# Recurrence outputs formed transposed, two heads at a time in the two halves of the array, with the chunk decay sent through DRAM

## The chip, the cores and the metric

The kernel runs on one core of one Trainium2 chip. The metric is the device time of one execution in microseconds (us). Before the change the median of 3 runs is 918.32 us (907.49 to 930.42).

## The reference, cut to what matters

Two parts follow each other. A gated linear recurrence runs over 4 sequences of 768 steps with 8 heads of 48 elements; its output, 3072 tokens of 384 elements, goes through a two-level top-1 mixture of 16 experts.

```python
# gated recurrence, per batch and head; a = a_re + i a_im, made at most 0.999 long
for t in range(S):
    S = a[t] * S + outer(k[t], v[t])        # S: 48 x 48, complex
    y[t] = q[t] @ real(S)
# mixture of experts over x = y by token, [3072, 384]
g = argmax(x @ w_group);  e = argmax(x @ w_expert[g])       # 4 groups of 4 experts
out = p_g * p_e * (relu(x @ w1[g, e]) @ w2[g, e])           # p: the softmax weights of the choice
```

All arrays are 32-bit floats; an expert's `w1` is 384 x 1024 and its `w2` 1024 x 384.

## The kernel before, in words

**Tiling.** The recurrence is worked off in 24 chunks of 128 steps, two chunks to a group, so 12 groups, three to a sequence. Within a chunk the decay and the turn of every step are running sums over the chunk (a product with a triangular matrix on TensorE); q and k are scaled and turned by them, and what is left are matrix products. A 96 x 384 state (`G`: cos and sin parts by 8 heads of 48) carries from chunk to chunk. The running sum of the log decay is measured from the middle of the chunk, so the state is multiplied by a half chunk's decay when it enters (`enter`, L405) and by the other half when it leaves (`leave`, L435).

**Steps of a group.** `gate_steps` (L285) makes the log decay (`ta`), the scales `E` and `Ei` (L311 to L320) and the angle (`tb`). Its step `decays` (L323) spreads `ta` over the cos and sin copies on GpSimd (L328) and multiplies each of 2 x 8 blocks with a 128 x 2 matrix `halves` on TensorE (L331), which gives the half chunks' decays in partitions; VectorE keeps their greatest (L334) and ScalarE takes the exponential `M` (L336). `turn_steps` (L352) makes sines and cosines and the products `Q` and `K`.

**Steps of a chunk** (`chunk_steps`, L396): `scores` transposes four heads of Q and K (L419, copied by ScalarE at L423 and VectorE at L425), multiplies them into `at` (L428) and masks it into `am` on VectorE (L431). `leave` forms the new state (L440 to L448). `outputs` (L451) forms y as 128 tokens x 384: per head one matmul with the 128 x 128 `am` stationary and 48 columns of v moving (L456), and one with the 96 x 128 `QT` stationary and 48 columns of the entering state moving (L458). ScalarE copies y to `x` (L461) and at once sends it to `x_dram` (L463). `gating` transposes x in three blocks (L183 in `transposed`, called by `gate`), VectorE copies them to `xT` (L188), and three matmuls against `wg` give the logits (L191, L192). `route` (L204), a group later, chooses the experts and writes the table of tokens.

**Order of the work.** The five engines and the DMA queues each run their own instructions in order and wait on semaphores. A loop over groups calls `weave` (L18), which mixes the step lists of four groups by a fraction of the iteration; a scheduler of the framework then sets each engine's order. SyncE issues the loads of q, k, v, a_re, a_im, and of the first two experts' weights; ScalarE issues the writes of `x_dram`.

```python
for g in range(-1, NG):
    turn, product = turned(g + 1)
    main = [f for c in range(GC) for f in chunk_steps(g, c)] if g >= 0 else []
    weave((0.0, 1.0, main), (0.0, 0.6, gates(g + 2)), (0.1, 0.1, routed(g - 1)),
          (0.0, 0.5, turn), (0.61, 1.0, product))
```

So the scales and decays of a group are made two iterations before its chunks use them. After the last group a branch tests whether any half chunk decayed by more than `exp(-LIMIT)`; if so, a loop would step through the recurrence in time. It isn't entered with these inputs. Then come the experts, each with its first 256 tokens (L626 and L635), and a loop for tokens beyond.

Of the kernel before, what the change touches and what calls it, by code (L numbers as in the profile page):

```python
# [10 lines left out]
F32 = mybir.dt.float32  # L11
# [16 lines left out]
def tile_gateloop_moe(  # L28
# [43 lines left out]
    NP = H // 2                 # head pairs  # L72
# [3 lines left out]
    LIMIT = 27.0  # L76
# [22 lines left out]
    table = dp.tile([NE * N, 2], I32, name="table")  # L99

# [9 lines left out]
    halves = cp.tile([P, 2], F32, name="halves")  # L110
    nc.vector.memset(halves, 0.0)
    nc.vector.memset(halves[0:64, 0:1], 1.0)
    nc.vector.memset(halves[64:128, 1:2], 1.0)
    lmat = cp.tile([P, P], F32, name="lmat")
    nc.vector.tensor_scalar(out=lmat, in0=ut, scalar1=-1.0, scalar2=halves[:, 0:1], op0=ALU.mult, op1=ALU.add)
# [12 lines left out]
    wg = cp.tile([P, KD, NW], F32, name="wg")  # L128
    nc.scalar.dma_start(out=wg[:, :, 0:G], in_=w_group.rearrange("(i p) g -> p i g", p=P))
    for g in range(G):  # L130
        nc.scalar.dma_start(out=wg[:, :, G + g * Eg:G + (g + 1) * Eg],
                            in_=w_expert[g].rearrange("(i p) e -> p i e", p=P))
# [12 lines left out]
    # counted[e] is how many tokens so far chose expert e; empty slots of the table name row N,  # L145
    # which is zero and has no row of the result.
# [11 lines left out]
    decay_max = cp.tile([P, GC * H * 2], F32, name="decay_max")  # L158
    nc.vector.memset(decay_max, 0.0)
# [19 lines left out]
    def transposed(x, evac):  # L179
        """[128 tokens, DM] -> [128 d, KD, 128 tokens]."""  # L180
# [5 lines left out]
    def gate(x, gl, c):  # L186
        xT = rp.tile([P, KD, P], F32, tag="xT", name="xT")
        transposed(x, lambda tp: nc.vector.tensor_copy(out=xT, in_=tp))  # L188
        lg = bank("sm", [P, NW])
        for i in range(KD):  # L190
            nc.tensor.matmul(out=lg, lhsT=xT[:, i, :], rhs=wg[:, i, :], start=(i == 0), stop=(i == KD - 1))  # L191
        nc.vector.tensor_copy(out=gl[:, c, :], in_=lg)  # L192

    def choose(logits, sh, oh):
        """oh: one-hot of the first greatest logit; sh: logits less the greatest."""
# [8 lines left out]
    def route(g, gl):  # L204
# [14 lines left out]
        # weight: 1 / (sum of the groups' exponentials) / (sum of the experts')  # L219
# [9 lines left out]
        # rank within the expert: earlier tokens of the chunk, earlier chunks, earlier groups  # L229
# [55 lines left out]
    def gate_steps(g):  # L285
        """Scales, decays and angles of a group."""
# [14 lines left out]
        def log_decay():  # L301
            # nl = ln(mag + 1e-6) - ln(mag) - min(ln(mag), ln(0.999)), the gate's -log magnitude
# [20 lines left out]
        def decays():  # L323
            # a half chunk's whole decay, by (cos and sin x d, head)
# [395 lines left out]
```

## Time and profile before

| | |
|---|---|
| median of 3 runs | 918.32 us (907.49, 918.32, 930.42) |
| the profiled execution: span from first to last instruction | 922.2 us (what lies around the span is not listed for it) |
| TensorE (PE) busy | 801.3 us, 87% of the span |
| its weight loads (PEld) busy | 649.3 us, 70% |
| VectorE (DVE) busy | 412.0 us, 45% |
| ScalarE (ACT), GpSimd (POOL) busy | 208.9 us and 208.1 us, 23% each |
| mean granted clock of TensorE | 0.811 of full speed |

The span has three stages: a start of about 52 us, the recurrence from there to 519.6 us, and the experts from about 553 us, with a passage of 33 us between. A matmul of 32-bit floats stands in the trace as two records (x384 at L456 are 192 matmuls), a transpose as one. Records of one stream overlap, so a record's duration is longer than its distance to the next; "busy" in the table by stretch is the time in which at least one of the rows asked for was running. PEclk is the granted clock as a share of 2.4 GHz: 0.5 is 1.2 GHz, 1.0 is 2.4 GHz, and what lies between is a mean over a stretch.

### The profile page before, as it was taken

Reading aid. Unit: us, or ns where it says so; the run is one execution under the profiler, and the core shown is the slowest. Engines: PE = TensorE matmul, PEld = TensorE weight load, DVE = VectorE, ACT = ScalarE, POOL = GpSimd, SP = SyncE. Lnnn points to the kernel's source line nnn. Section 1 sums busy time; section 2 is a strip of 40 time slices with the busy share of each in tenths; the row PEclk is TensorE's granted clock in tenths of the full one; section 3 lists DMA queues with packets and bytes.
Section 4 is the critical chain, followed back from the end, with each engine's and each line's share of the span. In section 5 each row is a group of like instructions: output and inputs, shape, how many; then the busy total and the mean of one; then the engine's idle time right before and its main releaser. Section 6 shows DMA issues by size and latency. Waiting matters only on the chain. (4 is left out here: it accounts for less than half of the span.)

```text
span 922.2 us, 10483 instructions
## 1 busy us (share of the span) xinstructions
PE 801.3 (87%) x3953; PEld 649.3 (70%) x3953; DVE 412.0 (45%) x1019; ACT 208.9 (23%) x356; POOL 208.1 (23%) x214
## 2 busy tenths in 40 slices
PE   1578989899899999999999609999999999999994
PEld 0467878688878778788888507767777777777762
DVE  5486787857757757657563311121111111111110
ACT  2454434334242433342321100000000000000000
POOL 4541314313131503123010021122221111111000
PEclk9977677866656667576665659999999999999997
DMA  8812202122120203000000013455555554544400
GB/s 275 306 61 77 77 28 78 55 74 66 38 75 29 78 26 103 10 27 9 9 10 11 17 26 113 167 169 170 182 183 184 182 182 169 170 167 158 151 13 15
DMA packets 54011, 90.89 MB, mean 99 GB/s; under 512 B 10156, under 2 KB 45016, under 8 KB 53954
## 3 DMA queue, kind: packets, MB, share of 16 engines
q1 hardware_dynamic: 43488, 73.96, 24.5%
q0 software_dynamic: 4864, 11.04, 3.4%
q10 hardware_dynamic: 5602, 5.15, 1.6%
q8 instruction: 33, 0.54, 0.3%
q14 instruction: 24, 0.20, 0.1%
HBM read 80.28 MB, written 11.43 MB: 99 GB/s over the span
## 5 line engine op out<-in xcount | busy, mean ns | idle before, releaser
L626 PE MATMUL cs<-xgT,w 128*128 128x256 f32 x768 | 171.2, 383 | 8.1 <-DVE xgT L621 8.1
L626 PEld LDWEIGHTS cs<-xgT,w 128*128 128x128 f32 x768 | 145.5, 191 | 31.1 <-DVE xgT L621 11.7
L631 ACT ACTIVATE hT<-cs 128x256 f32<-128x256 f32 x64 | 24.6, 384 | 344.8 <-PE cs L626 344.8
L456 PE MATMUL y<-v,am 128*128 128x48 f32 x384 | 89.9, 336 | 9.3 <-DVE am L431 9.2
L456 PEld LDWEIGHTS y<-v,am 128*128 128x128 f32 x384 | 78.4, 256 | 19.7 <-DVE am L431 13.6
L629 DVE TENSOR_SCALAR hT<-cs 128x256 f32<-128x256 f32 x64 | 27.2, 425 | 144.9 <-PE cs L626 141.9
L428 PE MATMUL at<-QT,KT 96*128 96x128 f32 x384 | 82.3, 380 | 7.5 <-DVE am L431 2.4
L639 POOL DMA_INDIRECT out_dram<-ot,ent x32 | 32.5, 1014 | 242.2 <-DVE ot L638 238.2
L635 PE MATMUL at<-w,hT 128*128 128x384 f32 x256 | 85.2, 486 | 0.0
L635 PE MATMUL y<-w,hT 128*128 128x384 f32 x256 | 85.2, 486 | 0.0
L428 PEld LDWEIGHTS at<-QT,KT 96*128 96x128 f32 x384 | 71.9, 278 | 15.2 <-DVE KT L425 7.0
L458 PE MATMUL y<-Gp,QT 96*128 96x48 f32 x320 | 77.8, 332 | 0.0
L635 PEld LDWEIGHTS y<-w,hT 128*128 128x128 f32 x256 | 48.6, 190 | 33.9
L635 PEld LDWEIGHTS at<-w,hT 128*128 128x128 f32 x256 | 48.6, 190 | 30.5
L328 POOL COPY both<-ta 128x768 f32<-128x768 f32 x24 | 24.3, 1037 | 200.0 <-DVE mx L201 116.7
L458 PEld LDWEIGHTS y<-Gp,QT 96*128 96x128 f32 x320 | 64.8, 251 | 0.0
L314 PE MATMUL cs<-ta,lmat 128*128 128x384 f32 x48 | 33.4, 849 | 25.1 <-DVE ta L308 24.8
L246 POOL DMA_INDIRECT table<-pay,slot_i x24 | 27.7, 1152 | 117.9 <-DVE slot_i L244 52.8
L419 PE MATMUL tp<-ident,K 128*96 128x128 f32 x192 | 42.5, 359 | 9.9 <-ACT QT L423 9.9
L610 POOL DMA_INDIRECT xg<-x_dram,ent x32 | 32.8, 1024 | 62.5 <-PE tp L183 49.4
L423 ACT COPY QT<-tp 96x512 f32<-96x512 f32 x48 | 27.9, 582 | 77.1 <-PE tp L419 72.3
L431 DVE TENSOR_TENSOR am<-at,mask 128x512 f32<-128x512 f32 x48 | 33.1, 689 | 26.9 <-PE at L428 26.2
(143 smaller groups left out, 1150.5 us busy)
## 6 DMA issues: line engine op xcount, KB each, us to landing
w<-in_w_dram SPq DMA_DIRECT2D x32, 1536.0 KB, 7.3
ar<-in_a_re_dram SPq DMA_DIRECT2D x12, 384.0 KB, 4.2
ai<-in_a_im_dram SPq DMA_DIRECT2D x12, 384.0 KB, 3.7
q<-in_q_dram SPq DMA_DIRECT2D x12, 384.0 KB, 3.9
k<-in_k_dram SPq DMA_DIRECT2D x12, 384.0 KB, 4.8
v<-in_v_dram SPq DMA_DIRECT2D x12, 384.0 KB, 3.2
x_dram<-x ACTq DMA_DIRECT2D x24, 192.0 KB, 2.4
xg<-x_dram,ent POOLq DMA_INDIRECT x32, 5.0
```

What stands on the lines that cost most here:

```text
L246: nc.gpsimd.indirect_dma_start(out=table, out_offset=bass.IndirectOffsetOnAxis(ap=slot_i[:, c:c + 1], axis=0), in_=pay[:, c, :], in_offset ...
L314: nc.tensor.matmul(out=cs, lhsT=lmat, rhs=t["a"][:, c], start=True, stop=True)
L419: nc.tensor.transpose(out=tp[:, j, :], in_=T[nm, g, c][:, hg * 4 + j].rearrange("p u d -> p (u d)"), identity=ident)
L423: nc.scalar.copy(out=tr[nm][0:DD], in_=tp)
L428: nc.tensor.matmul(out=at[:, j, :], lhsT=tr["K"][0:DD, j, :], rhs=tr["Q"][0:DD, j, :], start=True, stop=True)
L431: nc.vector.tensor_tensor(out=am, in0=at, in1=mask4, op=ALU.mult)
L456: nc.tensor.matmul(out=yh, lhsT=z["am", hg][:, j, :], rhs=V(h), start=True, stop=first)
L458: nc.tensor.matmul(out=yh, lhsT=z["QT", hg][0:DD, j, :], rhs=z["Gp"][0:DD, h, :], start=False, stop=True)
L610: nc.gpsimd.indirect_dma_start(out=xg, out_offset=None, in_=x_dram, in_offset=bass.IndirectOffsetOnAxis(ap=idx, axis=0), bounds_check=N, o ...
L626: nc.tensor.matmul(out=h, lhsT=wa[:, i, f * P:(f + 1) * P], rhs=xT[:, i, :], start=(i == 0), stop=(i == KD - 1))
L635: nc.tensor.matmul(out=y, lhsT=hT[:, f, i * P:(i + 1) * P], rhs=wb[:, f, :], start=(f == 0), stop=(f == KF - 1))
L639: nc.gpsimd.indirect_dma_start(out=out, out_offset=bass.IndirectOffsetOnAxis(ap=entries[i][:, 0:1], axis=0), in_=ot, in_offset=None, bound ...
```

## The change

- The log decay is summed from the chunk's start (`lmat` is the negated triangular matrix alone), ScalarE reads the sums from PSUM without the clamp on VectorE, and `LIMIT` doubles.
- The last row of `E`, the decay of a whole chunk, is written to `decay_dram` by SyncE, and read back two times per group into the 96 partitions of `decay`, 48 x 16 single elements each. The GpSimd copies, the L331 matmuls, the greatest on VectorE and the exponential `M` are gone.
- The state is multiplied once, when it leaves; `enter` is gone.
- `outputs` forms y transposed: v (or the state) is stationary, 64 or 48 columns of it, and `am` (or `QT`) moves with 128 columns. The even head of a pair goes to partitions 0 to 63, the odd one to 64 to 111, so each uses one half of the array's columns. Per chunk it is 16 matmuls as before (8 in a sequence's first chunk).
- ScalarE copies 112 x 512 instead of 128 x 384. The logits come from this transposed form directly, with four matmuls against a `wg` that is laid out by pairs of heads, with zeros between.
- For `x_dram`, four transposes turn the copy back; VectorE copies them to `x`, and ScalarE's DMA follows that copy.

```diff
-    lmat: tensor_scalar(in0=ut, scalar1=-1.0, scalar2=halves[:, 0:1], op0=ALU.mult, op1=ALU.add)
+    lmat: tensor_scalar(in0=ut, scalar1=-1.0, scalar2=None, op0=ALU.mult)
...
-    wg = cp.tile([P, KD, NW], F32, name="wg")
-    nc.scalar.dma_start(out=wg[:, :, 0:G], in_=w_group.rearrange("(i p) g -> p i g", p=P))
+    wg = cp.tile([P, NP, NW], F32, name="wg")
+    nc.vector.memset(wg, 0.0)
+    for u in range(2):
+        rows = slice(u * 64, u * 64 + D)
+        nc.scalar.dma_start(out=wg[rows, :, 0:G], in_=w_group.rearrange("(n u d) g -> u d n g", n=NP, u=2)[u])
...
         def scales(c):
...
-                cl = tp_.tile([P, DM], F32, tag="cl", name="cl")
-                nc.vector.tensor_scalar(out=cl, in0=cs, scalar1=LIMIT, scalar2=-LIMIT, op0=ALU.min, op1=ALU.max)
                 for nm, sg in (("E", 1.0), ("Ei", -1.0)):
                     e = tp_.tile([P, DM], F32, tag=f"{nm}{c}", name=f"{nm}{c}")
-                    act(out=e, in_=cl, func=AF.Exp, scale=sg)
+                    act(out=e, in_=cs, func=AF.Exp, scale=sg)
                     T[nm, g, c] = e
+                nc.sync.dma_start(out=decay_dram[g * GC + c:g * GC + c + 1, :], in_=T["E", g, c][P - 1:P, :])
             return f
 
         def decays():
-            ms = bank("sm", [DD, GC * H, 2])
-            for c in range(GC):
-                both = pp.tile([P, H, 2, D], F32, tag="both", name="both")
-                nc.gpsimd.tensor_copy(out=both, in_=t["a"][:, c].rearrange("p (h d) -> p h d", d=D).unsqueeze(2)
-                                      .to_broadcast([P, H, 2, D]))
-                for h in range(H):
-                    nc.tensor.matmul(out=ms[:, c * H + h, :], lhsT=both[:, h].rearrange("p u d -> p (u d)"),
-                                     rhs=halves, start=True, stop=True)
-            dm = decay_max[0:DD].rearrange("p (a b) -> p a b", b=2)
-            nc.vector.tensor_tensor(out=dm, in0=ms, in1=dm, op=ALU.max)
-            M = st.tile([P, GC * H, 2], F32, tag="M", name="M", bufs=4)
-            act(out=M[0:DD], in_=ms, func=AF.Exp, scale=-1.0)
+            rows = decay_dram[g * GC:(g + 1) * GC, :].rearrange("c (h d) -> d (c h)", d=D)
+            with nc.allow_non_contiguous_dma(reason="rows to partitions"):
+                for u in range(2):
+                    nc.sync.dma_start(out=decay[u * D:(u + 1) * D, g * GC:(g + 1) * GC, :]
+                                      .rearrange("d c h -> d (c h)"), in_=rows)
...
         def leave():
+            z["G"] = T["G"] if not first else None
...
-            M2 = T["M", g][0:DD, c * H:(c + 1) * H, 1:2].to_broadcast([DD, H, D])
+            M = decay[0:DD, g * GC + c, :].unsqueeze(2).to_broadcast([DD, H, D])
...
         def outputs():
-            y = bank("y", [P, DM])
-            for h in range(H):
-                hg, j = divmod(h, 4)
-                yh = y[:, h * D:(h + 1) * D]
-                nc.tensor.matmul(out=yh, lhsT=z["am", hg][:, j, :], rhs=V(h), start=True, stop=first)
-                if not first:
-                    nc.tensor.matmul(out=yh, lhsT=z["QT", hg][0:DD, j, :], rhs=z["Gp"][0:DD, h, :],
-                                     start=False, stop=True)
-            x = st.tile([P, DM], F32, tag="x", name="x")
-            nc.scalar.copy(out=x, in_=y)
-            r0 = g * TG + c * P
-            nc.scalar.dma_start(out=x_dram[r0:r0 + P, :], in_=x)
+            y = bank("y", [P, NP, P])
+            vs = T["v", g][:, c]
+            gs = None if first else z["G"][0:DD].rearrange("p h d -> p (h d)")
+            for n in range(NP):
+                both = [(h, slice(u * 64, u * 64 + w), slice(h * D, h * D + w))
+                        for u, (h, w) in enumerate(((2 * n, 64), (2 * n + 1, D)))]
+                for h, rows, cols in both:
+                    nc.tensor.matmul(out=y[rows, n], lhsT=vs[:, cols], rhs=z["am", h // 4][:, h % 4],
+                                     start=True, stop=first)
+                if not first:
+                    for h, rows, cols in both:
+                        nc.tensor.matmul(out=y[rows, n], lhsT=gs[:, cols], rhs=z["QT", h // 4][0:DD, h % 4],
+                                         start=False, stop=True)
+            xT = st.tile([P, NP, P], F32, tag="xT", name="xT")
+            nc.scalar.copy(out=xT[0:PR], in_=y[0:PR])
+            z["xT"] = xT
 
         def gating():
+            xT = z["xT"]
+            tp = bank("tp", [P, NP, P], 2)
+            for n in range(NP):
+                nc.tensor.transpose(out=tp[:, n, 0:PR], in_=xT[0:PR, n, :], identity=ident[0:PR, 0:PR])
+            x = st.tile([P, NP, 2, D], F32, tag="x", name="x")
+            nc.vector.tensor_copy(out=x, in_=tp.rearrange("p n (u r) -> p n u r", u=2)[:, :, :, 0:D])
+            r0 = g * TG + c * P
+            nc.scalar.dma_start(out=x_dram[r0:r0 + P, :], in_=x.rearrange("p n u d -> p (n u d)"))
...
-            gate(z["x"], T["gl", g], c)
+            lg = bank("sm", [P, NW])
+            for n in range(NP):
+                nc.tensor.matmul(out=lg, lhsT=xT[0:PR, n, :], rhs=wg[0:PR, n, :], start=(n == 0), stop=(n == NP - 1))
+            nc.vector.tensor_copy(out=T["gl", g][:, c, :], in_=lg)
```

The changed kernel's lines carry other numbers: L311 is the sum of the log decay, L316 the write to `decay_dram`, L323 the read into `decay`, L440 and L444 the output matmuls, L447 ScalarE's copy, L454 the transposes back, L456 VectorE's copy, L458 the DMA to `x_dram`, L463 the logits.

On TensorE, the outputs of a chunk begin behind the transposes of its second four heads (`tp<-ident,K`) and the scores (`at`). `y` is the output bank, `am` the masked scores, `QT` the transposed q, `Gp` or `G` the state. Before:

```order
L419 MATMUL tp<-ident,K_558 96x128 x4
L428 MATMUL at<-QT,KT 128x128 x4
L456 MATMUL y<-v,am 128x48
L458 MATMUL y<-Gp,QT 128x48
L456 MATMUL y<-v,am 128x48
```

Now, in the first chunk of a middle group (a row is the output's partitions x columns; 64 and 48 partitions are the two halves):

```order
L407 MATMUL at<-QT,KT 128x128 x4
L398 MATMUL tp<-ident,K_826 96x128 x4
L440 MATMUL y<-am,v 64x128
L440 MATMUL y<-am,v 48x128
L444 MATMUL y<-QT,G 64x128
L444 MATMUL y<-QT,G 48x128
```

The two kinds alternated per head; now each kind comes as a pair of halves, and the next pair of heads follows.

On TensorE, the end of a group's first chunk before, from its last outputs to the next chunk's scores (`sm<-halves,both` are the decays, `tp<-ident,x` and `sm<-wg,xT` the gating):

```order
L458 MATMUL y<-Gp,QT 128x48
L360 MATMUL cs<-tb,tmat 128x384
L362 MATMUL cs<-f_726,last 128x384
L183 MATMUL tp<-ident,x 128x128 x3
L419 MATMUL tp<-ident,Q_598 96x128 x4
L331 MATMUL sm<-halves,both 96x2 x16
L419 MATMUL tp<-ident,K_602 96x128 x4
L191 MATMUL sm<-wg,xT 128x20 x3
```

Now:

```order
L444 MATMUL y<-QT,G 48x128
L454 MATMUL tp<-ident,xT 128x112 x4
L398 MATMUL tp<-ident,Q_867 96x128 x4
L311 MATMUL cs<-ta,lmat 128x384 x2
L398 MATMUL tp<-ident,K_871 96x128 x4
L398 MATMUL tp<-ident,Q_867 96x128 x2
L347 MATMUL cs<-tb,tmat 128x384
```

The sixteen decay matmuls are gone, there is one transpose more, and the logits (`sm<-wg,xT`, x4) come some rows later.

On ScalarE, the copy of the outputs and the DMA to `x_dram` in a middle group before:

```order
L176 ACT_TABLE_LOAD
L461 COPY x<-y 128x384
L463 DMA x_dram<-x 128x384
L423 COPY QT<-tp 96x512
L173 ACTIVATE ta<-ta 128x768
L173 ACTIVATE tb<-ta 128x768
```

Now:

```order
L181 ACT_TABLE_LOAD
L447 COPY xT<-y 112x512
L402 COPY QT<-tp 96x512
L178 ACTIVATE ta<-ta 128x768
L458 DMA x_dram<-x 128x384
L178 ACTIVATE tb<-ta 128x768
```

The DMA stands two instructions later, behind a wait for VectorE's copy of `x`.

## Rows read from the trace of the kernel before

**Rows 1.** Busy time by stretch of the span: stretch, length, each engine's busy us
```profile
core 0: us, PE busy (x) PEld busy (x) DVE busy (x) ACT busy (x) POOL busy (x), PEclk, DMA share, GB/s
52.00:106.80 54.80, 50.41 (x324) 43.52 (x323) 40.05 (x93) 22.10 (x36) 14.12 (x13) 0.78 0.15 47
106.80:434.60 327.80, 301.67 (x1717) 261.60 (x1715) 230.43 (x576) 119.99 (x195) 93.11 (x89) 0.68 0.18 54
454.90:519.60 64.70, 60.86 (x346) 56.01 (x344) 30.11 (x104) 11.76 (x20) 4.54 (x6) 0.66 0.03 10
```

**Rows 2.** Waits in 106.8 to 434.6 us: engine line <- released by: us, times, longest
```profile
DVE xT L188 <- PE tp L183: 19.3, 8, 4.7
...
PEld tp L419 <- ACT QT L423: 13.2, 16, 1.1
...
PEld y L456 <- DVE am L431: 9.5, 11, 1.2
```

**Rows 3.** Busy time by stretch, instructions on tile y alone (PE, PEld, DVE, ACT)
```profile
106.80:434.60 327.80, 78.33 (x464) 77.15 (x464) 0.00 (x0) 7.67 (x16) 0.68 0.18 54
454.90:519.60 64.70, 22.46 (x128) 21.45 (x128) 0.00 (x0) 1.44 (x4) 0.66 0.03 10
```

**Rows 4.** The same, instructions of line 428 alone (PE, PEld)
```profile
106.80:434.60 327.80, 56.07 (x256) 48.60 (x256) 0.68 0.18 54
```

**Rows 5.** The same, line 331 alone
```profile
106.80:434.60 327.80, 22.86 (x256) 23.07 (x256) 0.68 0.18 54
```

**Rows 6.** The same, line 183 alone
```profile
106.80:434.60 327.80, 12.34 (x48) 9.03 (x48) 0.68 0.18 54
```

**Rows 7.** The same, line 191 alone
```profile
106.80:434.60 327.80, 19.47 (x96) 19.65 (x96) 0.68 0.18 54
```

**Rows 8.** Timeline, start of a chunk's outputs: start, us, engine line
```profile
250.36 0.66 PE L456 MATMUL y<-v,am 128*128 128x48 f32 x2 [0.78 <-DVE am L431]
...
250.74 0.55 PEld L458 LDWEIGHTS y<-Gp,QT 96*128 96x128 f32 x2
...
250.82 0.63 PE L458 MATMUL y<-Gp,QT 96*128 96x48 f32 x2
...
251.25 0.63 PE L456 MATMUL y<-v,am 128*128 128x48 f32 x2
```

**Rows 9.** Timeline, TensorE, outputs of a later chunk
```profile
281.67 0.39 PE L456 MATMUL y<-v,am 128*128 128x48 f32 x2
281.89 0.39 PE L458 MATMUL y<-Gp,QT 96*128 96x48 f32 x2
```

**Rows 10.** Granted clock (PEclk) of these two stretches
```profile
250.30:253.80 3.50, 3.44 (x16) 3.45 (x17) 3.50 (x13) 0.00 (x0) 0.00 (x0) 0.50 0.01 2
281.60:283.40 1.80, 1.80 (x19) 1.80 (x18) 1.74 (x3) 0.00 (x0) 0.00 (x0) 1.00 0.05 9
```

**Rows 11.** By stretch: ahead of, during and after one burst of line 331
```profile
431.10:434.50 3.40, 2.98 (x18) 1.91 (x16) 2.60 (x7) 1.05 (x3) 3.29 (x3) 1.00 0.00 0
434.50:437.90 3.40, 2.92 (x34) 2.92 (x35) 1.42 (x7) 0.43 (x1) 0.00 (x0) 1.00 0.02 5
437.90:454.90 17.00, 16.22 (x69) 14.71 (x69) 9.94 (x20) 5.22 (x9) 2.16 (x3) 0.50 0.04 12
```

**Rows 12.** By stretch, the sum over ten stretches at full clock (88.4 us)
```profile
sum 88.40, PE 79.19 PEld 70.54 DVE 67.65 ACT 18.88 POOL 21.20; mean PE 7.92 PEld 7.05 DVE 6.76 ACT 1.89 POOL 2.12
```

**Rows 13.** Groups by line: busy us, mean ns of one | idle before, releaser
```profile
L428 PE MATMUL at<-QT,KT 96*128 96x128 f32 x384 | 82.3, 380 | 7.5 <-DVE am L431 2.4 <-DVE KT L425 2.0 <-DVE sh L198 1.9
L456 PEld LDWEIGHTS y<-v,am 128*128 128x128 f32 x384 | 78.4, 256 | 19.7 <-DVE am L431 13.6 <-issue 4.2
L316 DVE TENSOR_SCALAR cl<-cs 128x384 f32<-128x384 f32 x24 | 13.3, 555 | 17.7 <-PE cs L314 17.6
L410 DVE TENSOR_TENSOR Gp<-G,M 96x384 f32<-96x384 f32 x20 | 10.9, 546 | 0.0
L334 DVE TENSOR_TENSOR decay_max<-sm,decay_max 96x32 f32<-96x32 f32 x12 | 2.2, 186 | 23.3 <-PE sm L331 23.3
```

**Rows 14.** DMA issues: count, KB each, median us from issue to landing
```profile
x_dram<-x ACTq DMA_DIRECT2D x24, 192.0 KB, 2.4
...
wg<-in_w_expert_dram ACTq DMA_DIRECT2D x4, 6.0 KB, 4.4
```

More of the change, by code (lines that the diff above doesn't have):

```diff
@@ L75, in tile_gateloop_moe @@
     MAXOV = (N - CAP + P - 1) // P
-    LIMIT = 27.0
+    LIMIT = 54.0
+    PR = 64 + D
     TINY = 2.0 ** -60
@@ L99, in tile_gateloop_moe @@
     table = dp.tile([NE * N, 2], I32, name="table")
+    decay_dram = dp.tile([NG * GC, DM], F32, name="decay_dram")
     ident = cp.tile([P, P], F32, name="ident")
@@ L109, in tile_gateloop_moe @@
     nc.vector.memset(ones, 1.0)
[L110 to L113, printed above, removed]
     lmat = cp.tile([P, P], F32, name="lmat")
-    nc.vector.tensor_scalar(out=lmat, in0=ut, scalar1=-1.0, scalar2=halves[:, 0:1], op0=ALU.mult, op1=ALU.add)
+    nc.vector.tensor_scalar(out=lmat, in0=ut, scalar1=-1.0, scalar2=None, op0=ALU.mult)
     tmat = cp.tile([P, P], F32, name="tmat")
@@ L127, in tile_gateloop_moe @@
     nc.vector.memset(eps, 1e-6)
-    wg = cp.tile([P, KD, NW], F32, name="wg")
-    nc.scalar.dma_start(out=wg[:, :, 0:G], in_=w_group.rearrange("(i p) g -> p i g", p=P))
-    for g in range(G):
-        nc.scalar.dma_start(out=wg[:, :, G + g * Eg:G + (g + 1) * Eg],
-                            in_=w_expert[g].rearrange("(i p) e -> p i e", p=P))
+    wg = cp.tile([P, NP, NW], F32, name="wg")
[3 more added lines that the diff above has]
+        nc.scalar.dma_start(out=wg[rows, :, 0:G], in_=w_group.rearrange("(n u d) g -> u d n g", n=NP, u=2)[u])
+        for g in range(G):
+            nc.scalar.dma_start(out=wg[rows, :, G + g * Eg:G + (g + 1) * Eg],
+                                in_=w_expert[g].rearrange("(n u d) e -> u d n e", n=NP, u=2)[u])
     down_i = cp.tile([P, G], I32, name="down_i")
@@ L157, in tile_gateloop_moe @@
     clear_routes()
-    decay_max = cp.tile([P, GC * H * 2], F32, name="decay_max")
-    nc.vector.memset(decay_max, 0.0)
+    decay = cp.tile([P, NG * GC, H], F32, name="decay")
     chain = {"on": True, "at": None}
@@ L184, in transposed @@
         evac(tp)
[L186 to L192, printed above, removed]
     def choose(logits, sh, oh):
@@ L403, in V @@
             return T["v", g][:, c, h * D:(h + 1) * D]
-        def enter():
-            if first:
-                return
-            Gp = st.tile([P, H, D], F32, tag="Gp", name="Gp")
-            M1 = T["M", g][0:DD, c * H:(c + 1) * H, 0:1].to_broadcast([DD, H, D])
-            nc.vector.tensor_tensor(out=Gp[0:DD], in0=T["G"][0:DD], in1=M1, op=ALU.mult)
-            z["Gp"] = Gp
         def scores(hg):
@@ L441, in leave @@
                                  start=True, stop=True)
-            M2 = T["M", g][0:DD, c * H:(c + 1) * H, 1:2].to_broadcast([DD, H, D])
-            Gn = st.tile([P, H, D], F32, tag="G", name="G")
+            M = decay[0:DD, g * GC + c, :].unsqueeze(2).to_broadcast([DD, H, D])
+            Gn = st.tile([P, H, D], F32, tag="G", name="G", bufs=3)
             if first:
-                nc.vector.tensor_tensor(out=Gn[0:DD], in0=d, in1=M2, op=ALU.mult)
+                nc.vector.tensor_tensor(out=Gn[0:DD], in0=d, in1=M, op=ALU.mult)
@@ new lines, in outputs, with gating @@
+            xT = st.tile([P, NP, P], F32, tag="xT", name="xT")
+            nc.scalar.copy(out=xT[0:PR], in_=y[0:PR])
+            z["xT"] = xT
+        def gating():
+            xT = z["xT"]
[4 more added lines that the diff above has]
+            nc.vector.tensor_copy(out=x, in_=tp.rearrange("p n (u r) -> p n u r", u=2)[:, :, :, 0:D])
@@ L462, in outputs @@
             r0 = g * TG + c * P
-            nc.scalar.dma_start(out=x_dram[r0:r0 + P, :], in_=x)
-            z["x"] = x
-        def gating():
+            nc.scalar.dma_start(out=x_dram[r0:r0 + P, :], in_=x.rearrange("p n u d -> p (n u d)"))
             if c == 0:
                 T["gl", g] = rp.tile([P, GC, NW], F32, tag="gl", name="gl")
-            gate(z["x"], T["gl", g], c)
-        return [enter, scores(0), scores(1), leave, outputs, gating]
+            lg = bank("sm", [P, NW])
+            for n in range(NP):
+                nc.tensor.matmul(out=lg, lhsT=xT[0:PR, n, :], rhs=wg[0:PR, n, :], start=(n == 0), stop=(n == NP - 1))
@@ L473, in gates @@
+            nc.vector.tensor_copy(out=T["gl", g][:, c, :], in_=lg)
+        return [scores(0), scores(1), leave, outputs, gating]
     def gates(g):
@@ L505, in tile_gateloop_moe @@
     far = cp.tile([P, 1], F32, name="far")
-    nc.vector.tensor_reduce(out=far[0:DD], in_=decay_max[0:DD], axis=AX.X, op=ALU.max)
+    nc.vector.tensor_reduce(out=far[0:DD], in_=decay[0:DD].rearrange("p a b -> p (a b)"), axis=AX.X, op=ALU.min)
     fp = bank("tp", [1, DD], 2)
@@ L591, in tile_gateloop_moe @@
         clear_routes()
+        w3 = sp.tile([P, KD, NW], F32, name="w3")
+        nc.scalar.dma_start(out=w3[:, :, 0:G], in_=w_group.rearrange("(i p) g -> p i g", p=P))
+        for g in range(G):
+            nc.scalar.dma_start(out=w3[:, :, G + g * Eg:G + (g + 1) * Eg],
+                                in_=w_expert[g].rearrange("(i p) e -> p i e", p=P))
         for g in range(NG):
@@ L596, in tile_gateloop_moe @@
             for c in range(GC):
-                gate(x[:, c], gl, c)
+                xT = rp.tile([P, KD, P], F32, tag="x3T", name="x3T", bufs=1)
+                transposed(x[:, c], lambda tp: nc.vector.tensor_copy(out=xT, in_=tp))
+                lg = bank("sm", [P, NW])
+                for i in range(KD):
+                    nc.tensor.matmul(out=lg, lhsT=xT[:, i, :], rhs=w3[:, i, :], start=(i == 0), stop=(i == KD - 1))
+                nc.vector.tensor_copy(out=gl[:, c, :], in_=lg)
             route(g, gl)
```

9 lines of the change are left out of this document (4 added, 5 removed).

## The prediction

> **What bounds the kernel now.** I read the stages first: busy time by stretch. In the middle of the recurrence, 106.8 to 434.6 us, PE is busy 301.67 of 327.80 us (92%) and DVE 230.43 (70%); ACT and POOL have 37% and 28% [rows 1]. Eight groups pass there, since the 256 records of line 331 in it [rows 5] are eight bursts of 2 x 8 matmuls with two records each. So a group takes 40.98 us, of which PE works 37.71 and waits 3.27, and DVE works 28.80. The waits of that stretch say what PE waits for: ACT's copy of QT (13.2 us) and DVE's `am` (9.5 us), never more than 1.2 us at a time [rows 2]. PE is the bound, with DVE second.
>
> Then the timeline and the clock. A pair of output records (one matmul) follows the last one after 0.43 us in a stretch at clock 0.5, that is 1.2 GHz, and after 0.22 us at 1.0, 2.4 GHz [rows 8 to 10]. Over the eight groups the clock is 0.68 [rows 1]: much of PE's work here runs at half speed, so the clock is worth as much as any edit. Before and during the last burst of line 331, whose matmuls move 2 columns each, it is 1.0, and for the 17 us behind the burst it is 0.5, with PE 95% busy there [rows 11]. PE was busy before the fall, but with matmuls that barely move a column.
>
> **The change part by part**, per group in the middle stretch.
>
> *Decays.* The L331 matmuls go: 22.86 / 8 = 2.86 us of PE [rows 5].
>
> *Outputs.* Before, 78.33 us for 464 records, 0.169 us each and 58 to a group: 9.79 us [rows 3]. A record now moves 128 columns, as in L428, which took 56.07 / 256 = 0.219 us [rows 4]. One half after the other that is 58 x 0.219 = 12.70 us, 2.91 more than now. If the two halves run side by side, two records share that time: 6.35 us, 3.44 less. No row shows two matmuls in one array. A floor from the other side: L428 comes in blocks of four matmuls with their ends exposed, while outputs come in longer runs; half of today's 9.79 is 4.90. I take 4.90 to 6.35, so that the sum goes by 5.6: the halves touch different output partitions, the loop alternates them, and nothing in the order stands between the two of a pair. 12.70 stays as the far end.
>
> *Gating.* One transpose more per chunk, 2 x 12.34 / 48 = 0.51 us, and one logit matmul more, 4 records x 19.47 / 96 = 0.81 us [rows 6, 7]: +1.32.
>
> PE per group at today's clock: 37.71 - 2.86 + 1.32 - 9.79 + 5.6 = 31.98 us (39.08 with the halves in turn).
>
> The Trainium skill speaks against side by side in one place: "TensorE: Matmul & The Clock Gate", section on packing small matmuls, says a weight load overlaps a running matmul only if their row groups differ. Both halves here use the same rows. The trace disagrees for the whole array: the load of L458 starts at 250.74, while the matmuls of L456 that began at 250.36 run until 251.02, on the same rows 0 to 95 [rows 8]. By that rule each record would show half of a 128-column load, 0.128 us x 58 = 7.4 us (half of 256 ns [rows 13]), and the outputs would come to 13.0 us; by the trace, to 5.6. I go by the trace. "TensorEngine Tiling (Array Packing)", key properties, says that a change of tiling mode drains the engine. Outputs and scores now alternate, four changes a chunk; at what a lone record takes beyond its share, 380 - 219 = 161 ns [rows 4, 13], an estimate is 96 x 0.161 = 15 us over the whole kernel. No run here shows it, and the sum below is without it.
>
> *DVE* loses the clamp (2 x 0.555), the greatest (0.19) and the entering multiplication (10.9 / 12 = 0.91) [rows 13]: 28.80 - 2.21 = 26.59 us. Its copy of `x` replaces that of `xT`, same shape. POOL loses its two copies; it has room already.
>
> *Clock.* The moving columns go from 48 to 128 in the outputs, and the burst after which the clock fell is gone. I expect a clock above 0.68, without a figure; at 0.80 PE's 31.98 us would be 27.2, at 1.0 21.7. Either way PE falls to DVE's level or under it, so the clock beyond that point is worth little.
>
> *Waits.* The decays now take two DMA steps, some 2.4 us each by the nearest landing [rows 14]; they are made two iterations ahead of their use, over 60 us, which hides them. Without that cover DVE would stand at the state multiplication for 4.8 us a group, and KT and `am` behind it. SyncE gets four issues more per group, two behind waits for ACT's exponentials; the loads queued behind have a group of slack. ACT's DMA to `x_dram` now waits for PE's transposes and DVE's copy; QT copies and exponentials are queued behind it and PE waits for QT. Bounds: nothing, since two ACT instructions stand between and ACT idles 63%; at most the longest wait of that copy, 4.7 us a chunk [rows 2]. I take nothing for the sum and make the rest a rival.
>
> *Start.* Two bursts go (5.7 us), ten small loads on ACT's queue replace five, with one landing of 4.4 us to lose [rows 14]. I take zero.
>
> **What is late next, and the sum.** With PE at or under DVE, a group is bound by DVE and the hand-overs. In the ten stretches at full clock DVE was 67.65 / 88.40 = 76.5% busy while PE was still 90% busy [rows 12]. With PE's load down I take 79%: 26.59 / 0.79 = 33.7 us a group, 7.3 less than 40.98. Ends: DVE at 90%, 29.6 us; PE still the bound at today's clock with the halves in turn, 39.08 + 3.27 = 42.4 us.
>
> Eight groups: -58 us. The stretch 52 to 106.8 at the same share (17.8%): -9.8. The last groups, 434.6 to 519.6, have no decays, so only the outputs count: half of 22.46 us [rows 3] less four chunks' gating (2.6) is -8.6, and some 2 us for the 20 us before: -10.6. Together -78. The experts and the passage to them are not touched. 922.2 - 78 = 844 us of span; the median of the runs lies 3.9 us under that span, so 840.
>
> **The rivals.**
> *Halves in turn.* The pairs don't overlap and the clock stays: PE goes to between 36.2 (today's output time) and 39.1 us, a group to 39.5 to 42.4, against 40.98. About 915 us: no change. For it: no row shows overlap. Against: even then the outputs' columns keep the array fuller, and each step of the clock gives some back (at 0.75 the group is down to 38 us, 890).
> *Drained halves (slower).* Each switch between the left and the right half empties the array, so each record costs what a lone one lasts, 0.380 us [rows 13]: 58 x 0.380 = 22.0 us, +10.7 us a group with the other terms, +128 us: 1046. It decides from (9.79 + 1.54) / 58 = 0.195 us a record; above that PE is worse off. Against it: alternating 96-row and 128-row matmuls already follow each other without a gap [rows 8, 9], and by the same section of the tiling page a change of tile alone doesn't drain.
> *ACT's queue.* The wait for `x` holds up QT: 24 chunks x 1.7 us = +40 us on the forecast: 880. The 4.7 us are for it, the idle ACT against it.
> *DVE almost gapless.* 29.6 us a group: -91 - 15 - 12 = 800 us of median. For it: the clock may stay at full speed throughout. Against: at full clock DVE was busy no more than 76.5% [rows 12].
>
> **How the numbers follow.** Chances: forecast (815 to 865) 0.54; halves in turn 0.13; ACT's queue 0.13; DVE almost gapless 0.12; drained halves 0.08. The range leaves out the slower case and half of the case of no change: 793 to 900. Faster by over 2% (about what a measurement of this kernel can tell from no change; under 900 us): forecast, gapless, most of ACT's queue and a quarter of halves in turn, 0.82; within 2% 0.10; slower 0.08.
>
> **What would show it.** Right: output records of the two halves start together or at half of today's distance; the clock of the recurrence clearly over 0.68; a group at 32 to 35 us with DVE near 80% busy; few PE waits on ACT. Wrong: the y tile takes as long as today per group; PE over 90% busy at an unchanged clock; DVE waiting for `decay`; QT late behind the DMA of `x`.

## The result, and the profile after

The changed kernel takes 831.36 us (median of 4 runs, 822.52 to 834.01), the kernel before 912.9 in the same comparison (median of 4, 907.43 to 930.42): a ratio of 0.910, 95% interval 0.903 to 0.918. The forecast was 840, in a range of 793 to 900. The profiled execution took 830.78 us, with a span of 828.9 against 922.2. Executions of one kernel differ with the granted clock (spans of 820.6 us at 0.905 to 832.1 at 0.886 among the four after), so the medians of the experiments, and all ratios, leave out those that were slow by it: two of the four of e8 below (949.6 and 950.3 us) and one of e12 (1184.2 us, at 0.554).

Busy time by stretch, in the columns of [rows 1]. 106.5 to 371.5 us is eight groups, from the first turn matmul (line 347) of the fourth group to that of the twelfth; 399.6 to 428.6 is the end of the recurrence.

```profile
core 0: us, PE busy (x) PEld busy (x) DVE busy (x) ACT busy (x) POOL busy (x), PEclk, DMA share, GB/s
51.00:92.00 41.00, 32.53 (x251) 26.71 (x249) 30.13 (x59) 15.28 (x23) 8.14 (x6) 0.83 0.22 68
106.50:371.50 265.00, 210.64 (x1500) 167.75 (x1498) 218.04 (x537) 113.95 (x183) 75.98 (x70) 0.82 0.22 61
399.60:428.60 29.00, 25.34 (x221) 20.99 (x220) 16.34 (x51) 5.58 (x9) 2.83 (x7) 0.88 0.04 15
```

The recurrence ends at 428.6 us in place of 519.6. A group takes 33.12 us: PE works 26.33 of it and waits 6.80, DVE works 27.25 (82%). In the kernel before, the second line of [rows 1] holds eight groups with as many output records (464 there [rows 3], 466 here): 40.98 us a group, 37.71 of PE and 3.27 of waiting. Two numbers of such a row belong together: PE's busy time times its clock is about the work, in us at full clock. It was 37.71 x 0.68 = 25.6 us a group and is 26.33 x 0.82 = 21.6. So the 7.9 us that a group has lost split into less work at the old clock (25.6 - 21.6 = 4.0, over 0.68: -5.9), a higher clock (21.6 / 0.68 - 26.33: -5.4) and more waiting (+3.5).

What PE waits for in these groups, by the view of [rows 2], but in the rows of PE itself where two of those are of its weight loads (PEld):

```profile
PE y L440 <- DVE am L410: 32.6, 20, 3.9
PE tp L398 <- ACT QT L402: 6.7, 10, 0.7
PE tp L454 <- ACT xT L447: 5.5, 8, 0.7
PE at L407 <- DVE KT L404: 2.1, 6, 0.3
```

The first two such rows of the kernel before, from 116.2 to 450.9 us:

```profile
PE tp L419 <- ACT QT L423: 9.4, 17, 0.7
PE y L456 <- DVE am L431: 6.8, 9, 1.0
```

DVE's `am` has become the first wait, in pieces of up to 3.9 us; nothing waits for the chunk decay in this view. The instructions on tile y, as in [rows 3], have gone from 0.169 us a record to 44.15 / 466 = 0.095:

```profile
106.50:371.50 265.00, 44.15 (x466) 34.19 (x464) 0.00 (x0) 9.36 (x16) 0.82 0.22 61
```

The timeline shows how, and beside it what the chunk waits for:

```profile
197.93 0.49 PE L440 MATMUL y<-am,v 128*64 128x128 f32 x4 [2.88 <-DVE am L410]
...
205.25 0.65 PE L444 MATMUL y<-QT,G 96*48 96x128 f32 x4
205.68 0.65 PE L440 MATMUL y<-am,v 128*48 128x128 f32 x4
...
243.80 0.43 PE L440 MATMUL y<-am,v 128*64 128x128 f32 x4
244.06 0.39 PE L444 MATMUL y<-QT,G 96*48 96x128 f32 x4
244.29 0.39 PE L440 MATMUL y<-am,v 128*48 128x128 f32 x4
244.51 0.39 PE L444 MATMUL y<-QT,G 96*48 96x128 f32 x4
```

A row now holds four records, both halves' matmuls, and the next follows after 0.43 us at half clock and 0.22 at full: the distance that one matmul had in [rows 8, 9]. Two go in the time of one, at either clock. The clocks of these places, and of what lies ahead of the first:

```profile
194.80:198.20 3.40, 0.52 (x8) 0.28 (x7) 3.40 (x8) 2.09 (x4) 2.32 (x3) 1.00 0.76 169
198.20:228.90 30.70, 26.78 (x145) 22.16 (x142) 19.80 (x48) 7.57 (x13) 3.48 (x4) 0.50 0.08 24
243.70:245.50 1.80, 1.70 (x24) 1.53 (x25) 1.80 (x5) 0.55 (x1) 0.13 (x1) 1.00 0.00 0
```

PE did 0.52 us of work in 3.40 us while it waited for `am`, and then had 1.2 GHz for 30.7 us, in which it was busy for 26.78 (87%). A stretch like it comes once more in the eight groups, from 300.6 to 331.3 us. The Trainium skill, "TensorE: Matmul & The Clock Gate", Part 1 on the HAM clock gate, says that the clock is throttled by default and that activity of the engine releases it. This trace agrees as far as the fall goes; why the clock stayed at 1.2 GHz for 30.7 us with PE busy for most of them, these rows don't show.

### The profile page after: what moved, and what is told of

It is laid out like the page before. It is cut to its first block, busy times and chain, and to the rows that moved or that the text cites. A ratio compares the mean times of both kernels' runs of the same rounds, so it can differ in the third digit from the quotient of the medians.

```text
span 828.9 us, 9902 instructions
## 1 busy us (share of the span) xinstructions
PE 668.6 (81%) x3641; PEld 508.2 (61%) x3641; DVE 400.3 (48%) x960; ACT 204.6 (25%) x344; POOL 188.4 (23%) x190
## 5 line engine op out<-in xcount | busy, mean ns | idle before, releaser
L440 PE MATMUL y<-am,v 128*64 128x128 f32 (+1 forms) x384 | 49.6, 335 | 37.1 <-DVE am L410 36.4
L407 PEld LDWEIGHTS at<-QT,KT 96*128 96x128 f32 x384 | 60.9, 233 | 19.6 <-issue 9.8
L372 POOL TENSOR_TENSOR Ei<-k,Ei 128x384 f32<-128x384 f32 x24 | 26.1, 1103 | 198.0 <-ACT Ei L178 190.3
L407 PE MATMUL at<-QT,KT 96*128 96x128 f32 x384 | 66.9, 324 | 3.8 <-DVE KT L404 2.3
L440 PEld LDWEIGHTS y<-am,v 128*64 128x64 f32 (+1 forms) x384 | 28.2, 154 | 50.9 <-DVE am L410 47.2
L347 PE MATMUL cs<-tb,tmat 128*128 128x384 f32 x48 | 30.2, 722 | 22.8 <-DVE tb L333 22.8
L447 ACT COPY xT<-y 112x512 f32<-112x512 f32 x24 | 14.0, 585 | 137.6 <-PE y L444 121.0
L643 DVE TENSOR_SCALAR ot<-at,ent 128x384 f32<-128x384 f32 x16 | 9.9, 618 | 75.8 <-PE at L640 75.8
L643 DVE TENSOR_SCALAR ot<-y,ent 128x384 f32<-128x384 f32 x16 | 9.9, 618 | 72.7 <-PE y L640 72.7
```

Source lines behind the costliest of these rows:

```text
L347: nc.tensor.matmul(out=cs, lhsT=tmat, rhs=T["angle", g][:, c], start=True, stop=first)
L372: nc.gpsimd.tensor_tensor(out=e, in0=T[src, g][:, c], in1=e, op=ALU.mult)
L407: nc.tensor.matmul(out=at[:, j, :], lhsT=tr["K"][0:DD, j, :], rhs=tr["Q"][0:DD, j, :], start=True, stop=True)
L440: nc.tensor.matmul(out=y[rows, n], lhsT=vs[:, cols], rhs=z["am", h // 4][:, h % 4], start=True, stop=first)
```

## The experiments

In the table, group, PE, waits and DVE are us in one of eight groups, taken in each profile as above; work is PE times clock. The row of before is [rows 1]. The stretches of e5, e7 and e8 hold 16 output records more than their eight groups have, and that of e9 24 more: 0.2 to 0.4 us of PE a group too much. Ratios are to the kernel before on the same chip.

| kernel | median us | ratio, 95% interval | group | PE | waits | clock | work | DVE |
|---|---|---|---|---|---|---|---|---|
| before | 912.9 | 1 | 40.98 | 37.71 | 3.27 | 0.68 | 25.6 | 28.80 |
| after | 831.4 | 0.910 [0.903, 0.918] | 33.12 | 26.33 | 6.80 | 0.82 | 21.6 | 27.25 |
| e1 halves in turn | 851.0 | 0.935 [0.918, 0.951] | 35.36 | 28.39 | 6.97 | 0.84 | 23.8 | 27.34 |
| e2 decays only | 943.7 | 1.032 [1.018, 1.047] | 42.95 | 36.91 | 6.04 | 0.63 | 23.3 | 26.68 |
| e3 outputs only | 841.9 | 0.922 [0.907, 0.938] | 34.56 | 30.31 | 4.25 | 0.80 | 24.2 | 28.62 |
| e4 KT on ScalarE | 832.5 | 0.913 [0.902, 0.924] | 34.34 | 28.09 | 6.25 | 0.80 | 22.5 | 26.63 |
| e5 more DVE | 831.5 | 0.906 [0.899, 0.914] | 34.04 | 26.27 | 7.77 | 0.80 | 21.0 | 29.14 |
| e6 more PE | 803.4 | 0.876 [0.866, 0.885] | 29.61 | 25.18 | 4.44 | 0.93 | 23.4 | 26.84 |
| e7 x on SyncE | 812.2 | 0.885 [0.878, 0.893] | 31.53 | 24.45 | 7.08 | 0.89 | 21.8 | 27.27 |
| e8 decays, burst back | 925.8 | 1.009 [0.995, 1.023] | 43.58 | 39.40 | 4.17 | 0.65 | 25.6 | 26.16 |
| e9 extra, 16 columns | 829.4 | 0.896 [0.887, 0.904] | 33.59 | 27.18 | 6.41 | 0.84 | 22.8 | 27.65 |
| e10 e6 and e7 | 815.5 | 0.882 [0.875, 0.890] | 31.16 | 25.90 | 5.27 | 0.89 | 23.0 | 27.03 |
| e11 e4, e6 and e7 | 802.1 | 0.866 [0.858, 0.874] | 31.06 | 25.77 | 5.30 | 0.89 | 22.9 | 26.01 |
| e12 e4 and e6 | 822.6 | 0.898 [0.881, 0.915] | 32.32 | 26.96 | 5.36 | 0.89 | 24.0 | 26.91 |

**Halves in turn, decays alone, outputs alone.**

```diff
-            for n in range(NP):
-                both = [...]
-                for h, rows, cols in both:
+            for u, w in enumerate((64, D)):
+                for n in range(NP):
+                    h = 2 * n + u
```

> The kernel after, with the outputs of the four even heads first and those of the odd heads behind them, so that two neighbouring output matmuls always share one half of the array. Same matmuls, same counts. Theory (the halves of a pair run side by side): the y tile goes from 0.094 us a record to 0.17 to 0.20, from 5.6 to 10 to 11.6 us a group; PE from 27 to about 32 us a group of 34.1, so that PE's work no longer fits beside the waits for DVE: about +4 us a group, 870 us (850 to 890). Rival 1 (the records are short for another reason, such as the clock alone): 0.094 us a record still, 831 us. Rival 2 (DVE alone sets the end): y doubles, but PE's 7 us of waits in a group take it up: under 842 us.

In the same order of columns, tile y takes 64.83 us and the timeline goes back to one matmul (two records) in 0.43 us at half clock and in 0.22 at full:

```profile
108.30:391.20 282.90, 64.83 (x465) 54.77 (x464) 0.00 (x0) 9.38 (x16) 0.84 0.21 57
```
```profile
221.13 0.67 PE L440 MATMUL y<-am,v 128*64 128x128 f32 x4
...
222.44 0.63 PE L443 MATMUL y<-QT,G 96*48 96x128 f32 x2
222.87 0.64 PE L440 MATMUL y<-am,v 128*48 128x128 f32 x2
223.30 0.63 PE L443 MATMUL y<-QT,G 96*48 96x128 f32 x2
...
257.60 0.38 PE L443 MATMUL y<-QT,G 96*48 96x128 f32 x2
257.82 0.38 PE L440 MATMUL y<-am,v 128*48 128x128 f32 x2
258.04 0.38 PE L443 MATMUL y<-QT,G 96*48 96x128 f32 x2
```

The clocks of the two places:

```profile
211.60:225.00 13.40, 10.08 (x44) 8.32 (x45) 10.27 (x16) 2.49 (x4) 3.94 (x4) 0.50 0.11 30
256.40:259.00 2.60, 2.60 (x28) 2.41 (x27) 2.60 (x6) 0.10 (x1) 0.13 (x1) 1.00 0.00 0
```

So the halves do run side by side when neighbours lie in different halves: 64.83 against 44.15 us. That is 0.139 us a record, less than the 0.17 to 0.20 expected; two pairs still meet where the order goes from one half to the other (x4 at 221.13). But running side by side is worth only about 20 of the 81 us. The kernel with hardly any of it is at 0.935.

For the next, the outputs and the gating of before were put into the kernel after; for the third, the new outputs and gating into the kernel before:

```diff
-                    nc.tensor.matmul(out=y[rows, n], lhsT=vs[:, cols], rhs=z["am", h // 4][:, h % 4], ...)
+                nc.tensor.matmul(out=yh, lhsT=z["am", hg][:, j, :], rhs=V(h), start=True, stop=first)
```

> The kernel after with the outputs and the gating of the kernel before; what is left of the change is the log decay summed from the chunk's start and the chunk decay through DRAM. Theory by the prediction's terms at the old clock: 2.86 us of PE a group go, 37.7 to 34.9, group 41.0 to 38.1, about 12 groups in all: 885 us (875 to 893). Rival (the 2-column burst was what pulled the clock down): the middle of the recurrence goes from 0.68 to 0.78 or more, PE falls to DVE's level, 850 us or less. Rival (the decays were free, hidden by other waits): 913 us.

> The kernel before with the outputs by pairs of heads and the new gating; the decays stay as 2-column matmuls, with the log decay measured from the chunk's middle. Theory by the prediction's terms at the old clock: outputs 9.8 to 5.6, gating +1.3, PE 37.7 to 34.8 us a group, 885 us (870 to 890). Rival (128 moving columns in place of 48 raise the clock): clock 0.78 or more in the middle of the recurrence, DVE's 28.8 us a group at 81% set the end, 35.5 us a group, 850 us. If both parts alone stay at 885, the 26 us that the whole change brings beyond their sum come from the clock that only both together raise.

The decays alone make the kernel slower by 1.8 to 4.7%, which none of the three theories had. Its eight groups, and its waits:

```profile
125.80:469.40 343.60, 295.31 (x1459) 257.17 (x1460) 213.43 (x539) 114.91 (x183) 72.01 (x70) 0.63 0.17 47
```
```profile
PE y L441 <- DVE am L415: 19.2, 9, 4.2
PE at L412 <- DVE am L415: 15.2, 7, 4.8
```

PE's work has gone down, from 25.6 to 23.3 us a group, but the clock fell from 0.68 to 0.63 and the waits grew from 3.27 to 6.04 us, most of it for `am`. The outputs alone give 0.922: nearly the whole gain, at a clock of 0.80, with the burst of 2-column matmuls still in.

Halves in turn against decays alone is the pair that says most. Both have as many output records in a group (465 in eight) at the same distances, nearly the same work (23.8 and 23.3) and nearly the same waits (6.97 and 6.04). They differ in what moves: 128 columns against 48, with V and G held in the array instead of `am` and QT (and in the gating that goes with it). The clock is 0.84 against 0.63, and the time 851 against 944 us. PE is busy for 28.39 us a group against 36.91, with no less work: the 7.6 us between their groups are the clock. Which of the differences the clock follows, these two runs don't tell apart.

**Does DVE set the end?** KT's copies to ScalarE (`if True:` in place of `if nm == "Q":`, so that both copies go there), and the products of K twice:

```diff
-                        nc.vector.tensor_tensor(out=o[:, :, i, :], ...)
+                        for again in range(2 if nm == "K" else 1):
+                            nc.vector.tensor_tensor(out=o[:, :, i, :], ...)
```

> The kernel after with the copies of KT out of PSUM on ScalarE in place of VectorE: 4 x 0.68 us a group leave DVE (27.6 to 24.9), 4 x about 0.58 are added to ACT. Theory (DVE and its order set the end since the change): at the same share of 81% a group goes from 34.1 to 30.8 us, about -3.3 x 10.5 groups: 796 us (785 to 815). Rival 1 (PE at its granted clock sets the end): 825 to 840 us. Rival 2 (QT and KT now leave one behind the other on ACT and the scores start later): PE's waits on ACT grow by 0.58 us four times a group, 831 to 855 us.

> The kernel after, with VectorE's two products that make the turned K done twice into the same tile: 4 x 0.55 us more a group on DVE, off the chain of the group that runs. Theory (DVE's work sets the end, at a share of 81%): +2.2 / 0.81 = 2.7 us a group, 860 us (850 to 868). Rival (PE at its clock sets the end and DVE counts only where PE waits for one of its results; taking 2.7 us of copies off DVE brought nothing): under 842 us, with DVE's share up from 81% to 87%.

1.9 us more of DVE a group (29.14) changes nothing: 831.5 us. The other edit is a weaker test than meant: it took 2.7 us of copies off DVE, but DVE's busy time fell by 0.6 (26.63 against 27.25), since some of its other instructions became longer (`r` of line 270 went from a mean of 0.71 to 1.10 us), and PE's wait only changed its name. In the kernel with KT's copies on ScalarE it is this one, for the turns' matmul, which now stands earlier in PE's order:

```profile
PE cs L347 <- DVE tb L333: 39.0, 9, 6.1
PE y L440 <- DVE am L410: 1.4, 4, 0.3
```

**More work for PE, and x's DMA on another queue.**

```diff
-                for h, rows, cols in both:
-                    nc.tensor.matmul(out=y[rows, n], ..., start=True, stop=first)
+                for r in range(2):
+                    for h, rows, cols in both:
+                        nc.tensor.matmul(out=y[rows, n], ..., start=True, stop=first or r == 0)
```

> The kernel after, with each output matmul on am issued twice (the second starts the sum anew, so the result is the same): 32 records more a group, some 3.0 us of PE at 0.094 us. Theory 1 (PE at its clock sets the end, nothing hides its work): +3.0 x 11 groups, 864 us (855 to 870). Theory 2 (what sets the clock is how many columns move; the extra matmuls move 128 each): the middle clock rises from 0.82 to 0.88 or more and pays for them: 820 to 840 us. Rival (DVE sets the end): the extra work lies in PE's waits, which end at the same time: 828 to 836 us at an unchanged clock.

> The kernel after, with the DMA of x to DRAM issued from SyncE's queue in place of ScalarE's. Theory (the wait for x on ACT holds up nothing that PE needs): 831 us, within 1%. Rival (ACT's queue behind the wait for x delays QT and the exponentials): 5 us or more less, and PE's 6.7 us of waits for QT in the middle stretch halve.

The kernel that issues 32 records more a group is the faster by 28 us, below the ranges of all three theories. Its eight groups and its first waits:

```profile
107.70:344.60 236.90, 201.40 (x1756) 163.98 (x1754) 214.75 (x536) 113.99 (x183) 79.99 (x69) 0.93 0.26 68
```
```profile
PE tp L398 <- DVE KT L404: 17.5, 11, 2.7
PE at L407 <- DVE KT L404: 8.6, 2, 4.3
...
PE y L441 <- DVE am L410: 1.3, 3, 0.4
```

The clock is 0.93, above what theory 2 asked for, and PE is busy for less time with more work. DVE is now 91% busy. Of the 3.5 us that a group lost, 1.2 are PE's busy time and 2.4 are waits: the wait for `am` is gone. The order of PE's and DVE's instructions changed with the edit, though, so that the added work and the new order can't be told apart by this run alone.

The other queue brought 19 us, against my theory, but not in the way of the rival either: PE's waits for QT stayed at 6.7 us, and those of a group at 7.1. What changed is the clock, 0.82 to 0.89, at the same work (21.6 and 21.8) and the same DVE (27.25 and 27.27). At the place where the kernel after lost 30.7 us to half clock, this one has:

```profile
194.00:197.30 3.30, 2.08 (x18) 1.75 (x16) 3.30 (x10) 3.10 (x6) 3.30 (x4) 1.00 0.88 208
197.30:204.10 6.80, 4.13 (x22) 3.20 (x23) 5.48 (x8) 0.56 (x1) 3.57 (x2) 0.50 0.20 58
204.10:228.00 23.90, 18.44 (x162) 14.94 (x160) 21.31 (x58) 11.96 (x20) 6.90 (x7) 1.00 0.35 84
```

The edit also moved a few matmuls in PE's order, those of line 347 among them, and results of DVE; which of these kept the clock up wasn't told apart.

**The burst put back, and extra matmuls that move little.** A burst of 2 x 8 matmuls a group, 2 columns each (32 records, as line 331 had), went into the kernel with the decays alone; and in the kernel with extra matmuls, the extra ones move 16 columns (`cc = slice(0, P if r else 16)` on out and rhs).

> The kernel with the decays of the change and the old outputs (944 us), with two bursts of 16 matmuls a group put back that move 2 columns each, on data at hand and read by nobody, so that only PE has the work of the burst again and DVE has none of the old decays. Theory (the burst, though it moves hardly a column, is work that keeps the clock up, and without it the granted clock fell from 0.68 to 0.62): back to 930 us or less, middle clock 0.67 or more. Rival 1 (the burst costs what it lasts, 2.9 to 3.2 us a group, and the lower clock comes from PE's longer waits for DVE's am, which another order brought): 965 to 980 us at a clock of 0.62 or less. Rival 2 (it fills PE's waits): 944 us.

> As the kernel with each am output matmul issued twice (803 us), but the extra ones move 16 columns in place of 128; the second of each writes the whole tile as before. As many records, the same waits. Theory (the columns moved hold the clock up): the middle clock falls back from 0.92 to 0.82 or less, and with the extra PE time the kernel is no faster than the kernel after: 828 to 860 us. Rival (the extra matmuls helped by where they stand: another order, am asked for later, no long wait for am): 798 to 812 us at a clock of 0.90 or more.

The first is not decided: 1.009 [0.995, 1.023] against 1.032 [1.018, 1.047] without the burst, at 0.65 against 0.63. It doesn't cost its 2.9 us a group, that much is plain; whether it only fills waits (4.17 us in place of 6.04) or holds the clock, these runs don't say. The second lost the gain: 829.4 us, with a clock of 0.84 where the theory had 0.82 or less:

```profile
109.60:378.30 268.70, 217.42 (x1780) 173.38 (x1779) 221.21 (x537) 114.04 (x183) 72.42 (x69) 0.84 0.23 60
```
```profile
PE y L442 <- DVE am L410: 23.0, 17, 3.9
```

It issues as many records a group as e6, whose extra ones move 128 columns in place of 16. 2.0 of the 4.0 us between their groups are PE's busy time (25.18 in e6 against 27.18), though e6 does slightly more work (23.4 against 22.8), and 2.0 are waits. The control isn't perfect, since the order on PE and DVE shifted in every group as well, and the wait for `am` came back with it. So the rival, that the extra matmuls helped by the order they brought, isn't ruled out.

**Put together.**

> The kernel after with both edits that made it faster: each am output matmul twice (128 columns both times) and the DMA of x on SyncE's queue. Theory (both removed the same thing, the long stretches at half clock, and what is left is DVE at 90% busy): no sum of the two gains, 798 to 808 us. Rival (they are separate costs): 803 - 19 = 784 us.

> As the run before (am matmuls twice, x on SyncE's queue), with the copies of KT on ScalarE too. Theory (with the clock up DVE's work does set the end, at 90% busy with 27.6 us of 30.4; 2.7 us less of it shorten a group by up to 2.7 us): 770 to 785 us. Rival 1 (the order in which PE waits for DVE sets the end, as when the copies were moved alone): 798 to 810 us. Rival 2 (ACT hands QT and KT over later, PE idles and the clock falls): over 810 us.

> The kernel after with each am output matmul issued twice and the copies of KT on ScalarE, x's DMA on ScalarE's queue as in the kernel after. Beside the kernel with the extra matmuls alone (803 us, DVE 91% busy in the middle) it tells what DVE's 2.7 us a group are worth once the clock is up. Theory (there DVE's work sets the end): 770 to 790 us. Rival (what PE waits for moves from one result of DVE to the next, as in the two runs with the copies moved): 797 to 810 us, DVE's share down to about 84%, a new wait for tb of 3 us or more a group.

The two faster edits together (815 us) are no better than either: 12 us behind the extra matmuls alone. With the KT copies on ScalarE as well it is 802 us, as fast as the extra matmuls alone (803) and the fastest seen, and without the queue's edit 823, outside both ranges expected for it. So the gains don't add: the same KT edit goes with 13 us less beside both others and with 19 us more beside the extra matmuls alone. DVE's time a group stays between 26.0 and 27.0 in all of these, and PE waits again for the turns' angle, here in the kernel with all three:

```profile
PE cs L347 <- DVE tb L333: 31.5, 8, 6.6
```

## Why the prediction was right, and where not

The number was near and the bookkeeping of PE's work held, but two steps behind it were wrong, the worth of the clock and what bounds a group. That it came so near is in part luck, as the points on what is late next and on the ends say.

- *Outputs, 9.79 to 5.6 us a group: right.* 44.15 / 8 = 5.52, by halves that run side by side. The two figures are of stretches at different mean clocks, but at equal clock the distances in the timeline have halved. A record takes 0.095 us, which leaves nothing of the halves that drain each other (0.380). The price of the rival, 12.70 us in turn, was wrong: it came from the scores' records, and nearly in turn the outputs take 64.83 / 8 = 8.1 us at a clock of 0.84, or 10.0 at 0.68. A record that moves 128 columns follows the last after the same time as one of 48 [rows 8, 9].
- *PE's sum, 31.98 us at the old clock: right.* 31.98 x 0.68 = 21.7 us of work; measured 21.6.
- *Clock: the step that failed.* The prediction expected more than 0.68, which came true, and called the clock worth little once PE is at DVE's level or under it, which did not. The kernel after is at that point (PE 26.33 us a group, DVE 27.25, clock 0.82), and from there the queue's edit took another 19 us with the same work on both engines, at 0.89. Up to that point the clock is worth 5.4 us of a group's 7.9, and the pair of kernels with 128 and 48 columns puts 93 us between two that do nearly the same work. The rival of halves in turn was priced at 915 us for the same reason: with nearly all of the overlap gone and the clock up it is 851.
- *Decays, -2.86 us: right as work, wrong as a gain.* The rows behind the last burst [rows 11] were read as the burst pulling the clock down. With the burst gone and the outputs and gating of before kept, the clock is lower still (0.63) and the kernel 3.2% slower. Beside the new outputs the decays' part is worth some 10 us (0.922 to 0.910, with intervals that overlap, so not shown).
- *DVE's 26.59 us: 27.25.* The three instructions went, and some of those left became longer (below).
- *What is late next, DVE at 79% and 33.7 us a group: measured 82% and 33.12, but not as a bound by DVE's work.* 1.9 us more of it cost nothing, at 86%. The share of 79% was picked between 76.5% and 90%, and no run shows DVE's share as what sets a group's length: that 33.7 lay so near 33.12 is luck. PE's waits doubled to 6.80 us because single results of DVE stand late in its order, above all `am`, and the clock falls after such a wait, as at 198.2 us. Only where the clock stayed at 0.93 was DVE 91% busy; that kernel, with work added to PE, is at 803 us, the price of the rival with DVE almost gapless.
- *Waits on the chunk decay, none: right. ACT's queue, nothing:* the queue's edit is worth 19 us, but not through QT, which was the rival's path.
- *Start, end and passage:* the recurrence ends 91.0 us earlier, where 78 were forecast: the eight groups 62.8 in place of 58, what lies before and behind them 28.2 in place of 20.4. The experts' 369 us didn't move. So the span is 828.9 us in place of 844, 15 us off. The median is only 9 us off, because the prediction put it 3.9 us under the span, as it was before the change, and it lies 2.5 us above: luck again.

What stays open is why the granted clock differs between these kernels, and what a group's length follows from in each of them. Every edit of one part also moved where DVE's results stand against PE's requests, and differences of 10 to 20 us among the fast variants can't be put down to one cause by these runs.

## What to carry to other kernels

Multiply PE's busy time by its granted clock before you compare two stretches: it tells less work from the same work done faster, and here about half of the gain was the second. Of the two ways to write a product of small matrices, try the one in which the wide side moves, even where the number of instructions and their distance stay the same (851 against 944 us here, by a clock whose cause stays open). And price a part of a change by a run of that part alone, because removing work can cost time.

## What the runs showed of the hardware

**More matmuls, less time.** With 32 added records a group that move 128 columns the kernel was 28 us faster, at a clock of 0.93 in place of 0.82; with as many that move 16 columns nothing can be told (829.4 against 831.4 us). The order of the instructions differs too, so this is what was seen and not its cause.

**A DVE instruction beside a POOL product gets longer, to that product's end or beyond.** The cast of `slot_i`, two columns, lasts 155 to 169 ns in the eight cases of the kernel after that lie alone and 953 to 959 in the four beside a POOL product; the last operation on the angle (line 333) 942 to 946 alone and up to 2737. One such place, the line of POOL first, then DVE's, where the long `tb` (line 333) delays `KT` behind it:

```profile
198.23 1.47 POOL L291 TENSOR_TENSOR ta<-ar 128x768 f32<-128x768 f32 x1
```
```profile
196.25 0.15 DVE L241 CAST slot_i<-slot 128x2 int32<-128x2 f32 x1
196.32 0.95 DVE L332 SCALAR_TENSOR_TENSOR tb<-td,tb 128x768 f32<-128x768 f32 x1
197.19 0.68 DVE L410 TENSOR_TENSOR am<-at,mask 128x512 f32<-128x512 f32 x1
197.79 2.74 DVE L333 SCALAR_TENSOR_TENSOR tb<-td,tb 128x768 f32<-128x768 f32 x1
200.46 0.68 DVE L404 COPY KT<-tp 96x512 f32<-96x512 f32 x1
```

The Trainium skill, "SBUF — State Buffer", section "SBUF: two separate sides", says that DVE and GpSimd share one pair of ports, which one instruction holds to its end while the other stands. The trace agrees, with 0.16 us against 0.95 for the cast. Which of the two goes first isn't shown: line 333 here is recorded as starting 0.44 us ahead of the product, and still ends 0.83 us behind it. So DVE's load isn't a sum of fixed durations: with the KT copies on ScalarE, the cast is beside a product in 9 of 12 cases in place of 4, and its mean there is 822 ns.
